# Loading the parameters of a state-space layer in whole tensors, with five neighbouring channels per partition

## The chip, the core and the metric

The kernel runs on one core of a Trainium2 chip. A core has five engines that work on their own instruction queues in order: PE (TensorE, matrix products into the PSUM memory), DVE (VectorE, elementwise work), ACT (ScalarE, functions by table, and copies), POOL (GpSimd) and SP (SyncE, which here only issues DMAs). ACT and POOL issue DMAs too. The transfers of all queues are carried out by the same 16 DMA engines. The metric is the device time of one launch in microseconds (us), less is better.

## The reference

Two branches read the same x (2048 positions, 640 channels, bfloat16). Branch a is an attention with 32 heads over 8 positions at distance 2. Branch b is a long convolution per channel, whose filter K comes from a state-space model with 192 complex states per channel. A gate mixes them.

```python
g = sigmoid((x * gate_w).sum(-1))
a = attention(x, wqkv, wo)                  # window 8, dilation 2, 32 heads
dt = exp(log_dt)[:, None]                   # 640 channels
logdA = dt * (A_re + 1j * A_im)             # 640 x 192
dB = dt * (B_re + 1j * B_im)
P = exp(logdA[:, :, None] * l)              # l = 0..2047
K = einsum("dn,dnl,dn->dl", C, P, dB).real
b = irfft(rfft(x, 4096) * rfft(K, 4096))[:2048] + x * Dskip
out = g * a + (1 - g) * b
```

The six parameter tensors (real and imaginary parts of A, B and C) are 640 x 192 in bfloat16, 245,760 bytes each.

## The kernel before

**Parameters.** A partition holds five of the 640 channels. Channel d = 80a + 16k + b (a below 8, k below 5, b below 16) lies in partition 16a + b, place k. So the five channels of a partition are 16 apart in memory, and a load of one place k moves 128 rows of 384 bytes (`load`, L294 to L297). There are thirty such loads, on SP, ACT and POOL. Those of place 0 of all six tensors come first. `lg10` (L298) is a 10 x 128 tile with log_dt and gate_w, which a small PE product (L321) turns into columns; ACT takes exp of the one half (`dtb`, L322) and copies the other (`gw_sb`, L324). On SP's queue the first of four DMA transposes of x (`xl`, L65) stands between the loads of cim and of aim. POOL issues five loads of the attention weights (`wl`, L66).

**The two parts.** `part` (L326) works out, for a block of places, what the filter needs: logarithm of the size, angle by arctangent, and the two exponents, and writes them as sums of bfloat16 pieces into `Sprm` in DRAM. Part one has place 0 alone (tiles of 128 x 192), part two the places 1 to 4 (128 x 768). Its steps are named after what they do: `weights` (products of C and B), `phase` (A_im times dt, then `wrap` into one turn), `ratio`, `squares`, `size`, `signs`, `angle`, and the splits `st`, `sx`, `sl`, `sp`, `sa`. A split step (`piece`, L347) rounds a tile to bfloat16 on ACT (L352), issues its write on SP (L354, L356) and takes the rest on DVE (L358). Part one runs at once. Of part two, seven steps are issued before the chunk loop (L821), and the others one per tick of it (`tick_hook`, L840). The arctangent and the logarithm of part two are held back (`kg.between`) until the exponentials of chunk 0 are done, because each function needs its own table on ACT.

**The chunks.** Ten chunks of 16 channels per group make the filter. `load_L` (L451) reads pieces from `Sprm` with eight DMAs per chunk. PE forms arguments (`ar`, L480), ACT takes sines (`trg`, L491) and exponentials (`exq`, L498), DVE multiplies them (L521 to L523), PE sums over states (`kps`, L532). Chunk 0 starts with exponentials and goes on with sines. The ticks of this loop interleave the projection of x (`proj`, products on L116, evictions to `prj` on L118, stores on L120), the gate, and the attention (`core`). The attention's buffers lie in memory that the parameters give back when part two is done (`c1.close()`, then `load_wo`).

**The rest.** The filter is expanded, both filter and x go through a Fourier transform in two stages (L633, L720), are multiplied, and come back in two more (L749, L763). `chan(c, q)` says which column of a group's 160 channels belongs to chunk c and slot q; the inverse stage takes twenty groups of four columns (L744 to L753) in the chunk order and `x0` puts them in place.

**Order.** The program's scheduler places independent instructions of one engine by its own estimate of when they can start; within an engine they then run in that fixed order. `after` (L418) adds an order between two instructions without a semaphore.

Of the kernel before, what the change touches and what calls it, by code (L numbers as in the profile page):

```python
# [220 lines left out]
NST = 192  # L221
# [4 lines left out]
CQ = 8  # L226
NCH = 80 // CQ
# [10 lines left out]

def chan(c, q):

    return 8 * c + q


def _arg_consts():
# [36 lines left out]
class SSMParams:  # L281
# [5 lines left out]
    def loads(self, ctx, tc, A_re, A_im, B_re, B_im, C_re, C_im, log_dt, gate_w, ident, gw_sb, pa, xl, wl):  # L287

        nc = tc.nc
        self.pin = pin = ctx.enter_context(tc.tile_pool(name="sp_in", bufs=1))  # L290
        self.t = t = {}
        src = dict(cre=C_re, bre=B_re, cim=C_im, bim=B_im, aim=A_im, are=A_re)

        def load(eng, nm, k0, nk):  # L294
            t[nm, k0] = pin.tile([128, nk, NST], BF16, name=f"{nm}{k0}")
            for k in range(k0, k0 + nk):
                eng.dma_start(t[nm, k0][:, k - k0], src[nm].rearrange("(a k b) n -> k a b n", k=5, b=16)[k])  # L297
        lg10 = pin.tile([10, 128], BF16, name="lg10")  # L298
        nc.sync.dma_start(lg10[0:5], log_dt.rearrange("(a k b) -> k a b", k=5, b=16))
        for nm in ("cre", "cim", "aim"):  # L300
            load(nc.sync, nm, 0, 1)
        for nm in ("bre", "bim", "are"):
            load(nc.scalar, nm, 0, 1)
        nc.sync.dma_start(lg10[5:10], gate_w.rearrange("(k p) -> k p", p=128))
        for nm in ("bre", "bim"):
            load(nc.scalar, nm, 1, 4)
        load(nc.sync, "cre", 1, 4)
        load(nc.sync, "cim", 1, 4)
        xl[0]()
        for w_ in wl:  # L310
            w_()
        load(nc.sync, "aim", 1, 4)
        load(nc.gpsimd, "are", 1, 4)
        for x_ in xl[1:]:
            x_()
        self.eps = pin.tile([128, 1], F32, name="eps")
        nc.vector.memset(self.eps[:], 1e-30)
        self.dtb = pin.tile([128, 5], BF16, name="dtb")
        self.dt2 = pin.tile([128, 5], F32, name="dt2")
        lt = pa.tile([128, 2, 512], F32, name="ar")  # L320
        nc.tensor.matmul(lt[:, 0, 0:10], lg10[:], ident[0:10, 0:10], start=True, stop=True)  # L321
        nc.scalar.activation(self.dtb[:], lt[:, 0, 0:5], ACT.Exp)  # L322
        nc.vector.tensor_tensor(self.dt2[:], self.dtb[:], self.dtb[:], ALU.mult)
        nc.scalar.activation(gw_sb[:], lt[:, 0, 5:10], ACT.Identity)  # L324

    def part(self, pool, tc, k0, nk, hold):  # L326

        nc = tc.nc
        SH = [128, nk, NST]
        cre, cim, bre, bim, are, aim = (self.t[n, k0][:] for n in ("cre", "cim", "bre", "bim", "are", "aim"))  # L330
# [5 lines left out]
        V, SCA = nc.vector, nc.scalar  # L336
# [5 lines left out]
        def wrap(dst, src, mul, tmp):  # L342
            V.tensor_scalar(tmp[:], src[:], float(mul / 65536.0), MAGIC, ALU.mult, ALU.add)
            V.tensor_scalar(tmp[:], tmp[:], MAGIC, 65536.0, ALU.subtract, ALU.mult)
            V.scalar_tensor_tensor(dst[:], src[:], float(mul), tmp[:], ALU.mult, ALU.subtract)

        def piece(cur, nxt, i):  # L347
            if pc1 is None:
# [13 lines left out]
            return [lambda i=i: piece(bufs[i], bufs[i + 1], i0 + i) for i in range(n)]  # L362
        TT = V.tensor_tensor
        def weights():
            TT(wr[:], cre, bre, ALU.mult)
            TT(t0[:], cim, bim, ALU.mult)
            TT(wi[:], cre, bim, ALU.mult)
            TT(t1[:], cim, bre, ALU.mult)
            TT(wr[:], wr[:], t0[:], ALU.subtract)
            SCA.activation(ax[:], wr[:], ACT.Abs)  # L370
            TT(wi[:], wi[:], t1[:], ALU.add)
            SCA.activation(ay[:], wi[:], ACT.Abs)

        def phase():
            TT(tau[:], aim, dtB, ALU.mult)
            wrap(tau, tau, U16, s0)

        def ratio():
            TT(t0[:], ax[:], ay[:], ALU.max)
            V.tensor_scalar(t0[:], t0[:], 1e-30, None, ALU.max)  # L380
            V.reciprocal(t0[:], t0[:])
            TT(t1[:], ax[:], ay[:], ALU.min)
            TT(t1[:], t1[:], t0[:], ALU.mult)
            hold(lambda: SCA.activation(at[:], t1[:], ACT.Arctan))
# [17 lines left out]
        def angle():  # L402
            q = float(np.pi / 4)
            S3 = V.scalar_tensor_tensor
            S3(t1[:], at[:], q, ax[:], ALU.subtract, ALU.mult)
            S3(t1[:], t1[:], q, wr[:], ALU.subtract, ALU.mult)
            S3(t1[:], t1[:], 2.0 * q, wi[:], ALU.add, ALU.mult)
            S3(at[:], t1[:], float(U16 / 124.0), tau[:], ALU.mult, ALU.add)
            wrap(at, at, 124.0, t1)
        st, sx, sa, sl, sp = split(tau, 0, 3), split(x1, 5, 3), split(xa, 3, 2), split(xl_, 10, 2), split(at, 8, 2)  # L410
        if nk > 1:
            return [weights, phase, squares, st[0], ratio, size, signs, st[1], st[2], lambda: wrap(x1, tau, 256.0, t0), sx[0], sx[1], sx[2],
                    sl[0], sl[1], angle, sp[0], sp[1], lambda: TT(xa[:], are, dtB, ALU.mult), sa[0], sa[1]]
        return [weights, phase, squares, st[0], ratio, size, signs, st[1], st[2], lambda: wrap(x1, tau, 256.0, t0), sl[0], sl[1], sx[0],
                sx[1], angle, sx[2], lambda: TT(xa[:], are, dtB, ALU.mult), sp[0], sp[1], sa[0], sa[1]]


def after(tc, later, earlier):  # L418
# [259 lines left out]
def fft_conv(ctx, tc, P, kx, gaS, out2d):  # L678
# [61 lines left out]
    with tc.tile_pool(name="ff_ps3", bufs=4, space=PSUM) as ps3, tc.tile_pool(name="ff_psr2", bufs=1, side="right") as psr2, \  # L740
# [44 lines left out]
def gated_mix_kernel(ctx, tc, A_x, A_wqkv, A_wo, B_A_re, B_A_im, B_B_re, B_B_im, B_C_re, B_C_im, B_log_dt, B_Dskip, gate_w, out):  # L785
# [37 lines left out]
    Dk = keep.tile([128, 160], BF16, name="Dk")  # L823
    nc.gpsimd.memset(Dk[:], 0.0)
    for g in range(4):
        nc.gpsimd.dma_start(Dk[32 * g:32 * g + 1], B_Dskip[160 * g:160 * g + 160].unsqueeze(0))
    Dk = Dk[:].rearrange("p (c x q) -> p c x q", c=2, q=CQ)
# [128 lines left out]
```

## Time and profile before

| what | value |
|---|---|
| time, three runs | 445.99, 449.24, 454.27 us; median 449.24 |
| the profiled execution | 449.92 us, span 448.1 us |
| busy PE, DVE, ACT, POOL (share of the span) | 336.5 (75%), 312.9 (70%), 324.8 (72%), 87.0 (19%) |
| weight loads of PE | 188.4 us (42%), beside the products |
| mean granted clock of PE | 0.926 of full speed |
| DMA moved | 58.80 MB, mean 131 GB/s |
| first product of the projection | 26.71 us |
| first exponential, first sine of chunk 0 | 52.05 us, 69.05 us |
| last Fourier products of chunk stage (L720) to the end | about 366 to 448 us |

The span runs from the first to the last instruction; the time has 1.8 us more around it. A row of a timeline gives start, length, engine, line, operation, tiles and count, and in brackets the idle time before it with what ended it. SPq, ACTq and POOL rows of the form DMA_DIRECT2D are issues, not the transfers: an issue can be long because its queue waits. A wait is put down to the release that came last.

### The profile page before, as it was taken

How to read it: one execution, taken by the hardware profiler on the slowest of the kernel's cores; microseconds unless marked ns; L12 is line 12 of the kernel's file. 1: busy time of each engine (PE TensorE's matmuls, PEld its weight loads, DVE VectorE, ACT ScalarE, POOL GpSimd, SP SyncE). 2: the span in 40 equal slices, each digit the busy share in tenths (PEclk: the TensorE clock that was granted, in tenths of full speed). 3: DMA queues.
4: the chain of work that ended last, by engine and by line, in shares of the span. 5: the costliest groups of instructions: out<-in, count | busy, mean ns of one | idle time of the engine just before them, and what ended most of it. 6: DMA issues, size and time to landing. Idle time of an engine off the chain costs nothing.

```text
span 448.1 us, 11301 instructions
## 1 busy us (share of the span) xinstructions
PE 336.5 (75%) x4806; PEld 188.4 (42%) x4806; DVE 312.9 (70%) x409; ACT 324.8 (72%) x485; POOL 87.0 (19%) x125
## 2 busy tenths in 40 slices
PE   0035867959988989799859998877867688995981
PEld 0012422424434435344325453534445565553871
DVE  0289937427998775767987759693545856999784
ACT  0258799847886788956838779968793649996784
POOL 8801211263130320231220210000000000000035
PEclk9995996988889999989998999989996979998897
DMA  7696443685455537182583641401207794213137
GB/s 238 138 178 169 147 130 121 178 246 160 115 146 134 135 85 180 58 228 68 186 233 103 187 144 25 115 11 16 77 1 220 264 177 86 82 37 119 71 67 170
DMA packets 66745, 58.80 MB, mean 131 GB/s; under 512 B 53303, under 2 KB 58599, under 8 KB 66439
## 3 DMA queue, kind: packets, MB, share of 16 engines
q1 hardware_dynamic: 56719, 29.26, 26.4%
q0 software_dynamic: 8176, 26.94, 21.0%
q10 hardware_dynamic: 1800, 1.88, 1.4%
q8 instruction: 37, 0.61, 0.6%
q14 instruction: 13, 0.11, 0.1%
HBM read 35.67 MB, written 19.77 MB: 124 GB/s over the span
## 4 chain that ended last, share of the span: by engine, by line
PE 36%; ACT 19%; DVE 13%; DMA 10%; issue 7%; POOL 1%; SPq 1%; ACTq 0%; POOLq 0%; DVEq 0%
PE tb L116 7%; PE tb L196 6%; PE fp L720 4%; PE tb L206 4%; PE ar L480 4%; DVE bufA L674 3%; DMA kc<-kS 3%; PE bp L633 3%; ACT exq L498 3%; ACT sp_u L723 2%; PE lg L163 2%; DVE prod L161 2%; ACT sp_k L723 2%; ACT prj L118 2%; ACT ga L207 2%
## 5 line engine op out<-in xcount | busy, mean ns | idle before, releaser
L491 ACT ACTIVATE trg<-ar 128x608 bf16<-128x608 int16 x120 | 76.9, 681 | 5.4 <-PE ar L480 4.8
L480 PE MATMUL ar<-Rarg,L 64*128 64x216 bf16 (+1 forms) x480 | 59.4, 285 | 16.3 <-ACT trg L491 9.8
L116 PE MATMUL tb<-bufA 128*128 128x512 bf16 x220 | 59.9, 403 | 2.3 <-ACT prj L118 1.4
L161 DVE TENSOR_TENSOR prod<-qc,kc 128x2048 bf16<-128x2048 bf16 x40 | 47.8, 1219 | 17.4 <-DMA L<-Sprm 7.9
L193 DVE TENSOR_TENSOR pv<-vc,asb 128x4096 bf16<-128x4096 bf16 (+1 forms) x24 | 45.7, 1928 | 19.7 <-DMA asb<-aS 17.2
L116 PEld LDWEIGHTS <-bufA 128*128 128x128 bf16 x300 | 33.4, 123 | 60.4 <-issue 40.8
L498 ACT ACTIVATE exq<-ar 128x864 bf16<-128x864 f32 x60 | 52.0, 904 | 0.5 <-PE ar L480 0.2
L196 PE MATMUL tb<-pv,ident 128*128 128x512 bf16 (+1 forms) x192 | 44.6, 372 | 3.6 <-DVE pv L193 1.8
L116 PE MATMUL lg<-bufA 128*128 128x512 bf16 x80 | 23.4, 429 | 26.7 <-DMA bufA<-in_A_x_dram 16.0
L532 PE MATMUL kps<-qq,pt 128*32 128x22 bf16 (+1 forms) x2560 | 37.5, 175 | 6.1 <-DVE E L884 2.3
L480 PEld LDWEIGHTS <-L 64*128 64x128 bf16 x480 | 22.1, 94 | 47.1 <-issue 42.4
L118 ACT ACTIVATE prj<-tb 128x512 bf16<-128x512 f32 x44 | 26.5, 601 | 21.0 <-PE tb L116 13.4
L532 PEld LDWEIGHTS <-pt 128*32 128x32 bf16 (+1 forms) x2560 | 25.2, 91 | 34.4 <-issue 26.2
L521 DVE TENSOR_TENSOR pt<-trg,exq 128x1024 bf16<-128x1024 bf16 x30 | 20.6, 686 | 20.2 <-ACT exq L498 10.4
L720 PEld LDWEIGHTS <-PHI 128*128 128x128 bf16 x256 | 24.8, 97 | 18.2 <-issue 8.1
L163 PE MATMUL lg<-prod,ind 128*32 128x512 bf16 x160 | 22.7, 417 | 11.5 <-DVE prod L161 8.0
L206 PE MATMUL tb<-wo_sb,oT 128*128 128x320 bf16 x160 | 26.9, 298 | 2.7 <-ACT ga L207 1.5
L196 PEld LDWEIGHTS <-ident 128*128 128x128 bf16 x192 | 18.7, 102 | 22.6 <-issue 11.2
L523 DVE TENSOR_TENSOR qq<-trg,exq 128x1408 bf16<-128x1408 bf16 x30 | 26.5, 884 | 0.0
L651 POOL DMA_DIRECT2D PHI<-c_phi x8 | 4.4, 548 | 112.6 <-PE fp L720 109.4
L197 ACT ACTIVATE oT<-tb 128x512 bf16<-128x512 f32 (+1 forms) x24 | 12.7, 529 | 18.0 <-PE tb L196 17.9
L207 ACT ACTIVATE ga<-tb,g_sb 128x320 bf16<-128x320 f32 x32 | 17.1, 534 | 9.1 <-PE tb L206 8.1
(182 smaller groups left out, 590.2 us busy)
## 6 DMA issues: line engine op xcount, KB each, us to landing
asb<-aS SPq DMA_DIRECT2D x8, 512.0 KB
PSI<-c_psi SPq DMA_DIRECT2D x8, 512.0 KB
PHI<-c_phi POOLq DMA_DIRECT2D x8, 384.0 KB, 3.6
L<-Sprm SPq DMA_DIRECT2D x80, 36.0 KB
kc<-kS POOLq DMA_DIRECT2D x8, 337.5 KB, 6.5
vc<-vS POOLq DMA_DIRECT2D x8, 337.5 KB, 5.8
qc<-qS POOLq DMA_DIRECT2D x8, 320.0 KB, 4.4
Usb<-in_A_x_dram POOLq DMA_DIRECT2D x4, 640.0 KB, 7.3
```

The lines of the kernel that those rows point to most:

```text
L116: nc.tensor.matmul(ppf, self.wq[:, kt, which * D + e:(which + 1) * D:5], self.xT[:, kt, c0:c0 + SC], start=(kt == 0), stop=(kt == NKT - 1))
L118: nc.scalar.activation(t[:, e % 2, :], ppf, ACT.Identity)
L161: nc.vector.tensor_tensor(prod[:], qc[:, e, :].unsqueeze(1).to_broadcast([128, W, C]), win(kc[:, e, :], 0, W, DIL, C), ALU.mult)
L163: nc.tensor.matmul(lg[32 * b:32 * b + 32], ind[:], prod[:, :, 64 * b:64 * b + 64], start=(e == 0), stop=(e == 4), skip_group_check=True, t ...
L193: nc.vector.tensor_tensor(pv[:, :, 0:n, :], for_e, asb[:].unsqueeze(2).to_broadcast([128, W, n, C]), ALU.mult)
L196: nc.tensor.matmul(op[:, 0:n, :], ident[:], pv[:, w, 0:n, :], start=(w == 0), stop=(w == W - 1))
L206: nc.tensor.matmul(apf[:, :320], oT[:, e, i * 128:(i + 1) * 128], wo_sb[:, e, hf * 320:(hf + 1) * 320], start=(e == 0), stop=(e == 4))
L480: nc.tensor.matmul(ar[:, g2, a0:a0 + ncol], L[rows, gp, sub, m0:m0 + 128], R[rows, c0:c0 + ncol], start=True, stop=True, tile_position=(64 ...
L491: ins = nc.scalar.activation(dst[:, 2 * gp:2 * gp + 2, sub, :], ar[:].bitcast(I16)[:, :, 0:2 * SW:2], ACT.Sin, scale=SCL)
L498: self.last = nc.scalar.activation(dst[:, 2 * gp:2 * gp + 2].rearrange("p g s n -> p g (s n)"), ar[:, :, 0:2 * EW], ACT.Exp)
L532: nc.tensor.matmul(kps[32 * g:32 * g + 32, c2, NM * ql:NM * ql + NM], pt[rows, 8 * g + ql, v, :], qq[rows, 8 * g + ql, v, :], start=(key n ...
L720: nc.tensor.matmul(fp[:, fl, 0:320].rearrange("p (c x) -> p c x", x=32), PHI[:, fl, kind, :], B[:, :, 2 * f1 + ri].rearrange("p c q g -> p ...
```

## The change

The channel order changes so that partition p holds the channels 5p to 5p + 4. A whole tensor then loads with one DMA of 128 rows of 1920 bytes. Six such loads stand on SP and ACT, three each; log_dt comes by a load of 128 rows of 10 bytes and needs no product; gate_w keeps the small product, and its load now follows the first transpose of x. The places 0 and 1 to 4 become slices of the loaded tiles. Those DVE instructions of part two that read inputs are ordered behind the last wrap of part one's `angle` (`behind`). The steps of part two come in another order, and two maxima in `ratio` become one instruction.

```diff
 def chan(c, q):
-    return 8 * c + q
+    return 40 * (c % 2) + 5 * q + c // 2
+
+def place(x):
+    return 8 * (2 * (x % 5) + x // 40) + x // 5 % 8
...
-        def load(eng, nm, k0, nk):
-            t[nm, k0] = pin.tile([128, nk, NST], BF16, name=f"{nm}{k0}")
-            for k in range(k0, k0 + nk):
-                eng.dma_start(t[nm, k0][:, k - k0], src[nm].rearrange("(a k b) n -> k a b n", k=5, b=16)[k])
...
+        def load(eng, nm, ap):
+            t[nm] = pin.tile([128, 5, NST], BF16, name=nm)
+            eng.dma_start(t[nm][:], ap.rearrange("(p k) n -> p k n", k=5))
+        ldt = pin.tile([128, 5], BF16, name="ldt")
+        lg5 = pin.tile([5, 128], BF16, name="lg5")
+        nc.sync.dma_start(ldt[:], log_dt.rearrange("(p k) -> p k", k=5))
+        load(nc.sync, "cre", C_re); load(nc.scalar, "bre", B_re)
+        load(nc.sync, "cim", C_im); load(nc.scalar, "bim", B_im)
+        load(nc.sync, "aim", A_im); load(nc.scalar, "are", A_re)
         for w_ in wl:
             w_()
-        load(nc.sync, "aim", 1, 4)
-        load(nc.gpsimd, "are", 1, 4)
+        xl[0]()
+        nc.sync.dma_start(lg5[:], gate_w.rearrange("(k p) -> k p", p=128))
         for x_ in xl[1:]:
             x_()
...
+        nc.scalar.activation(self.dtb[:], ldt[:], ACT.Exp)
+        nc.vector.tensor_tensor(self.dt2[:], self.dtb[:], self.dtb[:], ALU.mult)
         lt = pa.tile([128, 2, 512], F32, name="ar")
+        nc.tensor.matmul(lt[:, 0, 0:5], lg5[:], ident[0:5, 0:5], start=True, stop=True)
+        nc.scalar.activation(gw_sb[:], lt[:, 0, 0:5], ACT.Identity)
...
         def weights():
-            TT(wr[:], cre, bre, ALU.mult)
-            TT(t0[:], cim, bim, ALU.mult)
-            TT(wi[:], cre, bim, ALU.mult)
-            TT(t1[:], cim, bre, ALU.mult)
+            for dst, p, q in ((wr, cre, bre), (t0, cim, bim), (wi, cre, bim), (t1, cim, bre)):
+                after(tc, TT(dst[:], p, q, ALU.mult), behind)
...
         def ratio():
-            TT(t0[:], ax[:], ay[:], ALU.max)
-            V.tensor_scalar(t0[:], t0[:], 1e-30, None, ALU.max)
+            V.scalar_tensor_tensor(t0[:], ax[:], 1e-30, ay[:], ALU.max, ALU.max)
...
         if nk > 1:
-            return [weights, phase, squares, st[0], ratio, size, signs, st[1], ...]
+            return [weights, ratio, squares, size, phase, st[0], signs, st[1], ...]
...
-    psteps = prm.part(pB, tc, 1, 4, kg.between.append)
+    psteps = prm.part(pB, tc, 1, 4, kg.between.append, prm.last)
...
-                        nc.tensor.matmul(cp[:, c2, l, :], Y[64 * c2:64 * c2 + 64, ro, 4 * cb + l, :],
+                        nc.tensor.matmul(cp[:, c2, l, :], Y[64 * c2:64 * c2 + 64, ro, place(4 * cb + l), :],
...
-            x0 = chan(cb // 2, 4 * (cb % 2))
-            dst = C.rearrange("p x (c q) -> p x c q", c=2)[:, :, :, x0:x0 + 4]
+            dst = C.rearrange("p x (c q) -> p x c q", c=2)[:, :, :, 4 * cb:4 * cb + 4]
...
+    for c2_ in range(2):
+        nc.gpsimd.tensor_copy(Dk[:, c2_].rearrange("p (j s) q -> p j s q", s=2), Dn[:, 80 * c2_:80 * c2_ + 80].rearrange("p (s q j) -> p j s q", s=2, j=5))
```

`Dn` takes the place of `Dk` as the target of the Dskip loads, and the two POOL copies bring it into the new channel order. `self.last` is the last instruction of part one's `angle`; phase and the A_re product of part two are put behind it in the same way.

More of the change, by code (lines that the diff above doesn't have):

```diff
@@ L291, in loads @@
         self.t = t = {}
-        src = dict(cre=C_re, bre=B_re, cim=C_im, bim=B_im, aim=A_im, are=A_re)
-        def load(eng, nm, k0, nk):
-            t[nm, k0] = pin.tile([128, nk, NST], BF16, name=f"{nm}{k0}")
-            for k in range(k0, k0 + nk):
[L297 to L309, printed above, removed]
+        def load(eng, nm, ap):
[7 more added lines that the diff above has]
+        load(nc.sync, "aim", A_im); load(nc.scalar, "are", A_re)
         for w_ in wl:
             w_()
-        load(nc.sync, "aim", 1, 4)
-        load(nc.gpsimd, "are", 1, 4)
+        xl[0]()
+        nc.sync.dma_start(lg5[:], gate_w.rearrange("(k p) -> k p", p=128))
         for x_ in xl[1:]:
@@ L319, in loads, with part @@
         self.dt2 = pin.tile([128, 5], F32, name="dt2")
+        nc.scalar.activation(self.dtb[:], ldt[:], ACT.Exp)
+        nc.vector.tensor_tensor(self.dt2[:], self.dtb[:], self.dtb[:], ALU.mult)
         lt = pa.tile([128, 2, 512], F32, name="ar")
[L321 to L326, printed above, removed]
+        nc.tensor.matmul(lt[:, 0, 0:5], lg5[:], ident[0:5, 0:5], start=True, stop=True)
+        nc.scalar.activation(gw_sb[:], lt[:, 0, 0:5], ACT.Identity)
+    def part(self, pool, tc, k0, nk, hold, behind=None):
         nc = tc.nc
         SH = [128, nk, NST]
-        cre, cim, bre, bim, are, aim = (self.t[n, k0][:] for n in ("cre", "cim", "bre", "bim", "are", "aim"))
+        cre, cim, bre, bim, are, aim = (self.t[n][:, k0:k0 + nk] for n in ("cre", "cim", "bre", "bim", "are", "aim"))
         f = lambda nm: pool.tile(SH, F32, name=f"{nm}_{k0}")
@@ L344, in wrap @@
             V.tensor_scalar(tmp[:], tmp[:], MAGIC, 65536.0, ALU.subtract, ALU.mult)
-            V.scalar_tensor_tensor(dst[:], src[:], float(mul), tmp[:], ALU.mult, ALU.subtract)
+            return V.scalar_tensor_tensor(dst[:], src[:], float(mul), tmp[:], ALU.mult, ALU.subtract)
         def piece(cur, nxt, i):
@@ L374, in phase @@
         def phase():
-            TT(tau[:], aim, dtB, ALU.mult)
+            after(tc, TT(tau[:], aim, dtB, ALU.mult), behind)
             wrap(tau, tau, U16, s0)
         def ratio():
-            TT(t0[:], ax[:], ay[:], ALU.max)
-            V.tensor_scalar(t0[:], t0[:], 1e-30, None, ALU.max)
+            V.scalar_tensor_tensor(t0[:], ax[:], 1e-30, ay[:], ALU.max, ALU.max)
             V.reciprocal(t0[:], t0[:])
@@ L408, in angle @@
             S3(at[:], t1[:], float(U16 / 124.0), tau[:], ALU.mult, ALU.add)
-            wrap(at, at, 124.0, t1)
+            self.last = wrap(at, at, 124.0, t1)
         st, sx, sa, sl, sp = split(tau, 0, 3), split(x1, 5, 3), split(xa, 3, 2), split(xl_, 10, 2), split(at, 8, 2)
         if nk > 1:
-            return [weights, phase, squares, st[0], ratio, size, signs, st[1], st[2], lambda: wrap(x1, tau, 256.0, t0), sx[0], sx[1], sx[2],
-                    sl[0], sl[1], angle, sp[0], sp[1], lambda: TT(xa[:], are, dtB, ALU.mult), sa[0], sa[1]]
+            return [weights, ratio, squares, size, phase, st[0], signs, st[1], st[2], lambda: wrap(x1, tau, 256.0, t0), sx[0], sx[1], sx[2],
+                    sl[0], sl[1], angle, sp[0], sp[1], lambda: after(tc, TT(xa[:], are, dtB, ALU.mult), behind), sa[0], sa[1]]
         return [weights, phase, squares, st[0], ratio, size, signs, st[1], st[2], lambda: wrap(x1, tau, 256.0, t0), sl[0], sl[1], sx[0],
-                sx[1], angle, sx[2], lambda: TT(xa[:], are, dtB, ALU.mult), sp[0], sp[1], sa[0], sa[1]]
+                sx[1], angle, sx[2], lambda: after(tc, TT(xa[:], are, dtB, ALU.mult), behind), sp[0], sp[1], sa[0], sa[1]]
 def after(tc, later, earlier):
@@ L822, in gated_mix_kernel @@
         psteps.pop(0)()
-    Dk = keep.tile([128, 160], BF16, name="Dk")
-    nc.gpsimd.memset(Dk[:], 0.0)
+    Dk = keep.tile([128, 2, NCH, CQ], BF16, name="Dk")
+    Dn = keep.tile([128, 160], BF16, name="Dn")
+    nc.gpsimd.memset(Dn[:], 0.0)
     for g in range(4):
-        nc.gpsimd.dma_start(Dk[32 * g:32 * g + 1], B_Dskip[160 * g:160 * g + 160].unsqueeze(0))
-    Dk = Dk[:].rearrange("p (c x q) -> p c x q", c=2, q=CQ)
+        nc.gpsimd.dma_start(Dn[32 * g:32 * g + 1], B_Dskip[160 * g:160 * g + 160].unsqueeze(0))
+    for c2_ in range(2):
+        nc.gpsimd.tensor_copy(Dk[:, c2_].rearrange("p (j s) q -> p j s q", s=2), Dn[:, 80 * c2_:80 * c2_ + 80].rearrange("p (s q j) -> p j s q", s=2, j=5))
     kx = KExpand(ctx, tc, Dk)
```

## The prediction

> **What bounds the kernel now.** I read the slices first, then the chain of waits, then the timelines of the opening. The slices:
>
> ```profile
> PE   0035867959988989799859998877867688995981
> DVE  0289937427998775767987759693545856999784
> ACT  0258799847886788956838779968793649996784
> ```
>
> One slice is 11.2 us. From the third on, three engines share the load and none is full; in the first two PE does nothing and ACT almost nothing. Each engine works in its written order, so a later stage starts when the earlier one lets it. The change touches the opening, so its worth is read there. The chain of waits, followed back, ends in it:
>
> ```profile
> 54.16 0.78 ACT exq L498
> 63.45 1.28 ACT L384
> 67.76 1.28 ACT L491
> 82.31 6.83 DMA Sprm<-pc
> 91.57 5.87 DMA kc<-kS
> ```
>
> Columns are start, length, what. The first piece is an exponential of chunk 0. From there to the attention's first loads at 91.57 the chain runs over the parameters: their table loads (L384, L491), the write of the last piece, and loads into the memory that they free. So what comes before 54 us is waited for. The timelines of the opening (start, length, engine, line, tile) show how it is made:
>
> ```profile
> 3.80 7.27 SPq L297 DMA_DIRECT2D cre<-in_B_C_re_dram  x4
> 18.88 4.59 SPq L65 DMA_TRANSPOSE bufA<-in_A_x_dram  x1
> ...
> 43.80 7.57 SPq L458 DMA_DIRECT2D L<-Sprm  x16
> ```
> ```profile
> 18.44 1.28 ACT L322 ACT_TABLE_LOAD   x1 [18.44 <-DMA bim<-in_B_B_im_dram]
> ...
> 27.50 0.36 ACT L352 ACTIVATE pc<-s 128x192 bf16<-128x192 f32 x1 [1.11 <-DVE s L358]
> ...
> 52.05 0.89 ACT L498 ACTIVATE exq<-ar 128x864 bf16<-128x864 f32 x1
> ```
> ```profile
> 12.17 0.36 DVE L366 TENSOR_TENSOR t<-cim,bim 128x192 f32<-128x192 bf16 x1 [7.81 <-DMA bim<-in_B_B_im_dram]
> 23.99 0.96 DVE L367 TENSOR_TENSOR wi<-cre,bim 128x768 f32<-128x768 bf16 x1 [3.61 <-DMA bim<-in_B_B_im_dram]
> ```
>
> ACT and SP spend the opening issuing thirty small parameter loads: SP needs 7.27 us for four, and ACT gets to its first table load at 18.44. DVE then reaches a product of the second part (four channels) at 20.4 and stands 3.61 us for bim, with the first part's wrap behind it. The milestones that I carry are: ACT's second rounding of the first part (27.50), the end of that part (the last split at 41.1), the L loads (43.80), the first exponential (52.05), and, from the same view of ACT, the first sine at 69.05.
>
> ```profile
> 27.50:41.10 13.60, 5.09 (x14) 1.87 (x13) 13.60 (x34) 12.81 (x25) 0.31 (x1) 0.71 0.87 181
> 52.05:69.05 17.00, 10.05 (x55) 4.52 (x54) 8.11 (x10) 16.92 (x22) 1.99 (x3) 0.95 0.33 99
> ```
>
> Busy time in two stretches (PE, weight loads, DVE, ACT, POOL, clock, DMA share, GB/s): the first is bound by DVE, the second by ACT.
>
> **The loads.** Thirty loads of 128 x 384 bytes become six of 128 x 1920; the bytes stay 1.47 MB. The issues cost about 0.6 us each, so ACT has three instead of eleven and is free near 4 us instead of 18.4, SP near 3.3. Against that, the first part used 0.29 MB and now needs whole tensors, which arrive under the attention weights (2.46 MB, issued by POOL from 2.48 us). In the trace a packet of 384 bytes takes 22 ns, one of 1920 bytes (another load's) 89 ns and the weights' packets of 7680 bytes 313 ns. 768 x 89 and 320 x 313 over 16 DMA engines are 4.3 + 6.3 = 10.6 us, so all has landed at 13.1 if it starts at 2.5. The other bound is the rate of 4 to 12 us, 302 to 329 GB/s: 3.93 MB less 0.29 moved by 4 us, at 315, ends at 15.6. I take 14. For aim, last in its queue, I assume no place better than the end.
>
> How queues share the engines decides between the ends. The row is the first bim block: issued at 2.80, waited for until 12.17, though it is 128 packets, 0.2 us of sixteen engines. The Trainium skill (DMA: Bandwidth & Descriptors, Queues, rings and completion order) says that each DMA engine takes turns between queues a packet at a time, a packet being some 9 to 17 descriptors. By that a tensor's eight descriptors per engine would pass in one turn, and the third tensor of a queue would come three of the weights' long turns later: it speaks against the change, at the late end or beyond. No row here shows a turn's length.
>
> **x and the gate.** The first transpose of x now stands behind aim on SP's queue, and the gate weights (lg5) behind that transpose. The changed order shows more: PE's small product for the gate stands behind the first projection matmul, and its eviction gw_sb stands on ACT ahead of the first part's second rounding. So everything behind it on ACT (both table loads, all later splits) waits for x. That is a new wait. The transpose's packets took 4.8 us beside other loads and 2.9 to 3.6 alone; I take 3.2 after 14, then 1.5 us to the first matmul (packets ended at 25.2, PE began at 26.71) and 0.8 for two products and the eviction: gw_sb at 19.5, bounds 17.5 and 21.5. Before, ACT did that second rounding at 27.50. Meanwhile weights, phase and the wrap of the first part hide under the loads; with that cover gone they would cost some 3 us.
>
> **First part.** In the 13.60 us stretch DVE did 7.9 us of the second part (eight products or sums at 0.87 and two at 0.47, spaced). The new order puts all of these behind the first part, so 5.7 us of its own remain as the lower bound. But five projection evictions now stand between its splits on ACT, with PE groups of 1.24 to 2.3 us behind them, so the old 13.6 is the upper one. I take the middle, 9.6: end at 29.1. SP has issued the three other transposes by then (3.2 us each from 17.2 is 26.8). The writes and their landing cost 2.7 as before (41.1 to 43.80): L loads at 31.8.
>
> **First exponential.** Before it came 8.25 us after the L loads began, with PE ready after 6.5 (49.98 plus a product of 0.36) and an eviction and a table load in between that can now go earlier. I take 7.0: 38.8.
>
> **Exponential to first sine.** ACT is full there, 17 us, and now has more in it: nine projection evictions instead of six (0.49 each) and six roundings plus one sign instead of four plus one (0.8 each), 3.1 us; with PE's pace for groups in a row up to 5. I take 3.5: first sine at 59.3 instead of 69.05. The second part's own chain on DVE lies beside this: by its rows some 19 us of passes with the 4.86 us reciprocal, 5 for the next wrap and splits, 3 of waits for ACT's roundings, 27 in all; from 27 it is at its arctangent at 54.
>
> **Edits at nothing.** The fused maximum saves a pass (0.47) on an engine with slack there. The two Dk copies (80 columns each) sit on POOL between projection stores that wait for ACT anyway; their loads go out with those stores, with 5.6 us to land, ahead of the k stores, and exposed would cost up to 5 us of POOL. chan and place alter addresses only: same shapes, same strides, same counts. From the arctangent on, the order on every engine is the same in both kernels, table loads included (24), so I carry the gain to the end.
>
> **Sum.** 69.05 - 59.3 = 9.75 us. The profiled execution took 449.92 (span 448.1), 0.7 over the median 449.24: 440.2 against it; I say 440.0. The own range from gw_sb (2 each way), first part (up to 3.9) and exponential stretch (1.5), not all at one end, is 436 to 444.5.
>
> **Rivals.** (1) The parameters hardly wait for the weights: larger packets take more of every turn, aim is there at 11, gw_sb at 17, the splits run near their 5.7 plus two table loads of 1.28. Then the sine comes at 55 to 56, and the time is 435 to 437. For it: from 5 to 12 us the trace has 394 parameter packets of 384 bytes beside about 270 of the weights, so what a turn carries decides. Against: DMA was 98% busy from 8 to 12, so bytes must come from the weights, which the first projection needs. (2) The gain is absorbed: the attention's loads at 91.57 wait for the last write and wo, and the long middle is shared by three engines; 446 to 450. Against: identical orders. (3) Slower: the weights hold the whole tensors back, and with them x, the gate and all of ACT's queue, while "behind" forbids DVE to fill the gap with second-part work. Each us by which gw_sb comes after 19.5 takes one from the gain: nothing is won at 29.3, and over 2% (9 us) lost past 38. Three tensors follow each other on a queue; if each takes bim's 9.4 us, aim is there at 31 and gw_sb at 36.5, and with the slower ends of the later steps the time is 459 to 462. For it: that bim row. Against: the weights' last packet starts at 12.7 in this trace, and all bytes fit before 15.6. That the change does nothing is excluded, since thirty issues go.
>
> **How the numbers follow.** A measurement here can tell about 2% from no change (three runs spread from 445.99 to 454.27); faster means under 440.3. Forecast 0.60, just over half of it beyond the bound (0.34 faster, 0.26 same). Rival 1: 0.24, faster. Rival 2: 0.05, same. Rival 3: 0.11, slower. So 0.58, 0.31, 0.11. The range 434 to 449 takes in forecast and rival 1 with their bounds and part of rival 2, and leaves out some 0.15.
>
> **What would show it.** ACT's first table load near 4 us; the first wrap at 14 to 16; gw_sb directly after the first projection matmul, at 17.5 to 21.5; L loads at 30 to 34; first sine at 57 to 62. From there each milestone should keep its distance to the end: the last Fourier stages, 364 to 411 before, move by the same amount. I am wrong if aim lands after 18, if DVE rather than ACT is late at the second arctangent, or if the distance from sine to end changes by over 3 us.

## The result and the profile after

The changed kernel took 447.08 us (median of 20 runs, 440.33 to 454.24), the kernel before 450.79 (20 runs, 445.99 to 454.65). The ratio is 0.9897, its 95% interval 0.9854 to 0.994. So it is 3.7 us faster, less than 2% and less than half of the 9.75 us that were forecast. Three more series of both, made later (after5, after6 and after7), gave 5.2, 4.5 and 5.0 us between the medians, about half of the forecast. The profiled execution took 447.28 us, span 445.5.

A ratio here is of the faster runs of each kernel alone; where a single early run of the kernel before (442.25 and 441.07 us in two series) makes it leave out most of its others, medians of all runs are compared.

The slices of the profile after, 11.1 us each, granted clock of PE below:

```profile
PE   0458749788889897998659998797768589995980
DVE  4399673279998848679668759664557557998882
ACT  2478999649977989668329689788775468995882
PEclk9997959969999999899859999979996889998896
```

The first two slices are fuller now: DVE is busy for 0.4 of the first one, where it had nothing to do before, and PE starts in the second slice and not in the third. The chain of waits (start, length, what) begins with the transposes of x and still runs over the parameters to the attention's first loads; its last line here lies far behind the opening:

```profile
2.67 11.17 SPq L65
13.89 3.61 DMA lg<-in_gate_w_dram
...
58.74 1.28 ACT L485
...
73.88 5.47 DMA Sprm<-pc
...
82.08 6.42 DMA kc<-kS
...
212.80 11.60 DMA kc<-kS
```

The attention's loads come at 82.08 in place of 91.57, 9.5 us earlier. Before, the line that answers to the last one was this, in the same view:

```profile
223.12 7.71 DMA kc<-kS
```

There the load was 10.3 us later, but it took 3.9 us less. The opening in the timelines of SP, ACT and DVE (start, length, engine, line, tile; idle time in brackets):

```profile
2.67 11.17 SPq L65 DMA_TRANSPOSE bufA<-in_A_x_dram  x1
...
24.23 4.29 SPq L353 DMA_DIRECT2D Sprm<-pc  x5
30.80 7.49 SPq L452 DMA_DIRECT2D L<-Sprm  x16
```
```profile
2.64 1.28 ACT L317 ACT_TABLE_LOAD   x1 [2.64 <-issue]
...
17.77 0.18 ACT L321 ACTIVATE gw_sb<-ar 128x5 bf16<-128x5 f32 x1 [6.15 <-PE ar L320]
...
37.30 0.89 ACT L492 ACTIVATE exq<-ar 128x864 bf16<-128x864 f32 x1
...
60.04 0.68 ACT L485 ACTIVATE trg<-ar 128x608 bf16<-128x608 int16 x1
```
```profile
6.43 0.36 DVE L363 TENSOR_TENSOR t<-cim,bim 128x192 f32<-128x192 bf16 x1 [1.14 <-DMA bim<-in_B_B_im_dram]
...
8.08 0.36 DVE L370 TENSOR_TENSOR tau<-aim,dtb 128x192 f32<-128x192 bf16 x1
```

ACT's first table load is at 2.64 in place of 18.44, and DVE uses aim, the last tensor, at 8.08. The second row of ACT shows the new wait: it is for PE, whose first product waits for x. The first sine comes at 60.04 in place of 69.05.

To see where these 9 us went, I set the two traces against each other, instruction by instruction on DVE and ACT. The lead is 9 us at the first sine, 9.1 to 11.3 from 120 to 225 us of the time before, and 6.5 at 231. From there it goes on falling, to 4.1 at 340 us, and the closing of the kernel takes 1.4 more (below), so that the spans differ by 2.6. Two rows of DVE mark the large step, at 231. Before:

```profile
231.02 1.22 DVE L161 TENSOR_TENSOR prod<-qc,kc 128x2048 bf16<-128x2048 bf16 x1 [1.16 <-DMA kc<-kS]
```

After:

```profile
224.52 1.22 DVE L161 TENSOR_TENSOR prod<-qc,kc 128x2048 bf16<-128x2048 bf16 x1 [5.34 <-DMA kc<-kS]
```

The same product waits 5.34 us for its load in place of 1.16. Windows around it, the middle one from some 2 us behind the first of the filter's loads, show what it draws with it (us, then busy time of PE, weight loads, DVE, ACT and POOL, granted clock, DMA share, GB/s), after:

```profile
169.60:214.50 44.90, 39.38 (x603) 18.71 (x601) 34.79 (x51) 33.33 (x53) 10.75 (x14) 0.96 0.46 138
214.50:234.50 20.00, 11.47 (x206) 5.21 (x206) 12.11 (x15) 7.03 (x11) 2.58 (x3) 0.66 0.58 170
234.50:295.00 60.50, 53.43 (x917) 26.88 (x915) 47.24 (x51) 49.69 (x78) 5.42 (x8) 0.94 0.32 93
```

and before:

```profile
180.00:225.00 45.00, 39.47 (x620) 18.81 (x618) 35.42 (x52) 33.67 (x53) 10.76 (x14) 0.96 0.45 136
225.00:240.00 15.00, 9.66 (x206) 4.97 (x206) 11.34 (x14) 6.91 (x11) 2.58 (x3) 0.89 0.78 226
240.00:300.00 60.00, 52.84 (x921) 27.16 (x920) 47.33 (x52) 49.85 (x78) 5.42 (x8) 0.97 0.33 95
```

The same 206 products of PE take 20 us in place of 15, the stretches around them are alike, and PE was granted 0.66 of its clock there in place of 0.89. PE's busy time grew by only 1.8 us, so most of the 5 us is waiting.

What meets there: at the end of chunk 4 the expanded filter is read back with four loads kc<-Kx of 327 KB (two on ACT, two on SP, packets of 10,240 bytes), and the attention reads its next keys with kc<-kS on POOL (packets of 4,320 bytes). All are issued within 1.4 us. In the kernel before, kc<-kS is issued 0.42 us after the first kc<-Kx and ahead of SP's first one (0.56); in the changed kernel at 0.77, behind it. Its first packet then moves at 3.87 us in place of 2.45, and that of SP's first one at 3.51 in place of 3.99. The opposite order of two issues is 0.35 us of difference at POOL and 4 us at DVE in these two executions.

### The profile page after: what moved, and what is told of

It is laid out like the page before. It is cut to its first block, busy times and chain, and to the rows that moved or that the text cites. A ratio compares the mean times of both kernels' runs of the same rounds, so it can differ in the third digit from the quotient of the medians.

```text
span 445.5 us, 11261 instructions
## 1 busy us (share of the span) xinstructions
PE 338.7 (76%) x4806; PEld 188.3 (42%) x4806; DVE 314.8 (71%) x407; ACT 324.6 (73%) x485; POOL 87.8 (20%) x123
## 4 chain that ended last, share of the span: by engine, by line
PE 39%; ACT 21%; DVE 16%; DMA 13%; issue 5%; SPq 4%; POOL 1%; ACTq 0%; DVEq 0%; POOLq 0%
PE tb L116 8%; PE tb L196 6%; PE fp L714 4%; PE tb L206 4%; PE ar L474 4%; DMA kc<-kS 4%; DVE bufA L668 3%; PE bp L627 3%; SPq L65 3%; ACT sp_u L717 2%; PE lg L116 2%; PE lg L163 2%; DVE prod L161 2%; ACT sp_k L717 2%; ACT prj L118 2%
## 5 line engine op out<-in xcount | busy, mean ns | idle before, releaser
L474 PE MATMUL ar<-Rarg,L 64*128 64x216 bf16 (+1 forms) x480 | 60.9, 289 | 24.2 <-ACT trg L485 11.4
L116 PE MATMUL tb<-bufA 128*128 128x512 bf16 x220 | 61.5, 409 | 2.2 <-ACT prj L118 1.2
L193 DVE TENSOR_TENSOR pv<-vc,asb 128x4096 bf16<-128x4096 bf16 (+1 forms) x24 | 45.7, 1927 | 21.5 <-DMA asb<-aS 17.6
L196 PE MATMUL tb<-pv,ident 128*128 128x512 bf16 (+1 forms) x192 | 43.5, 365 | 3.8 <-DVE pv L193 2.0
L515 DVE TENSOR_TENSOR pt<-trg,exq 128x1024 bf16<-128x1024 bf16 x30 | 20.5, 685 | 18.5 <-ACT exq L492 10.4
L196 PEld LDWEIGHTS <-ident 128*128 128x128 bf16 x192 | 18.5, 101 | 22.5 <-issue 10.1
L197 ACT ACTIVATE oT<-tb 128x512 bf16<-128x512 f32 (+1 forms) x24 | 12.7, 529 | 20.6 <-PE tb L196 20.5
```

Source lines behind the costliest of these rows:

```text
L116: nc.tensor.matmul(ppf, self.wq[:, kt, which * D + e:(which + 1) * D:5], self.xT[:, kt, c0:c0 + SC], start=(kt == 0), stop=(kt == NKT - 1))
L193: nc.vector.tensor_tensor(pv[:, :, 0:n, :], for_e, asb[:].unsqueeze(2).to_broadcast([128, W, n, C]), ALU.mult)
L196: nc.tensor.matmul(op[:, 0:n, :], ident[:], pv[:, w, 0:n, :], start=(w == 0), stop=(w == W - 1))
L474: nc.tensor.matmul(ar[:, g2, a0:a0 + ncol], L[rows, gp, sub, m0:m0 + 128], R[rows, c0:c0 + ncol], start=True, stop=True, tile_position=(64 ...
```

## The experiments

**Chance or not.** First both kernels again, unchanged.

> The changed kernel once more, as it is, for a second profile. In its first profile the first sine of chunk 0 came 9.0 us earlier than before, the lead was 10.7 us at 225 us of the old time, and 4.2 of it went between 225 and 240: there one attention load (kc from kS, 12.80 to 24.52 after 200) took 11.6 us instead of 7.7 beside four filter loads (kc from Kx), and PE ran 13.7 us at half clock behind it. Theory 1 (the loss is a fixed consequence of the new timing): the same load takes 11 to 12 us again and the stretch from the seventh k store's load to the next attention score is as long as in the first profile, 20 us. Rival (the loss is a matter of chance per execution): the load takes 7 to 9 us in this profile, the lead after it is 9 to 10.5 us, and what is lost lies elsewhere or nowhere. First sine in both: 59.5 to 60.5 us.

> The kernel of before once more, for a second profile. Theory 1: the load of kc from kS at 223 us takes 7.5 to 8 us again, and stages keep the lengths of the first profile within 0.5 us. Rival (chance): this load varies here too, by 2 us or more, or half-clock stretches of PE lie elsewhere and move a stage by 2 us or more. First sine at 68.5 to 69.5 in both.

443.33 and 450.9 us. I take as measure the stretch from the 26th to the 31st of DVE's products `prod`: 22.7 us in the first execution of the changed kernel and 22.0 here, 18.6 in both of the kernel before. So the lengthening is no chance of one execution. The first sine of the kernel before came at 66.90 this time; the 69.05 on which the forecast stands was a late one.

**The gate.** Is `gw_sb` what the opening waits for, as the prediction has it?

```diff
+        nc.sync.dma_start(lg5[:], gate_w.rearrange("(k p) -> k p", p=128))
         load(nc.sync, "cre", C_re); load(nc.scalar, "bre", B_re)
...
-        nc.sync.dma_start(lg5[:], gate_w.rearrange("(k p) -> k p", p=128))
```

> One change to the changed kernel: the load of gate_w goes out on SP right behind log_dt, ahead of the parameters and x, so that the gate's product and the eviction gw_sb no longer wait for the first transpose of x (ACT stood 6.15 us for it). Opening: gw_sb before 11 us, the first part's end 5 to 6 us earlier than 28 us unless the three later transposes on SP hold its writes (they end at 24.1), then only about 3 us earlier: L loads at 26 to 28 instead of 30.8, first sine at 55 to 58 instead of 60.0. End: theory A (a lead of the opening is carried to the end, minus chance) gives a time 2 to 4 us below the changed kernel, 443 to 445; theory B (the middle takes a lead back, whatever its size) gives the changed kernel's time within 1 us.

`gw_sb` was written at 4.04 in place of 17.77, and little came of it: the first part's last rounding came 0.8 us earlier (27.05), the first sine 0.7 (59.39), the L loads later (31.17, not 30.80). The time was 447.62 us, ratio 0.9895 (0.9826 to 0.9964). ACT's timeline shows why:

```profile
4.04 0.16 ACT L321 ACTIVATE gw_sb<-ar 128x5 bf16<-128x5 f32 x1
...
14.16 0.36 ACT L349 ACTIVATE pc<-s 128x192 bf16<-128x192 f32 x1 [1.11 <-DVE s L355]
...
21.67 0.60 ACT L118 ACTIVATE prj<-lg 128x512 bf16<-128x512 f32 x1 [2.79 <-PE lg L116]
```

The second rounding is early now, but the first eviction of the projection stands on ACT ahead of the rest of the splits, and that waits for x as before. PE's first product came 1.6 us later here (18.32, not 16.73), so the two kernels differ in x too.

**The order of the two loads.** A semaphore is a counter by which one instruction waits for another. Each DMA of POOL signals its end on one of eight, taken in turn. The kernel before has four more DMAs on POOL (are) than the changed one, so all later ones have other semaphores. The load kc<-kS waits for five of them, one after the other, and where the last one to come (that of POOL's last store of keys) stands in that row decides when the load is issued. In the kernel before it stands last, and the load goes out 0.28 us after the store has landed (223.12 and 222.84); in the changed kernel it stands first, and the load goes out 0.63 us after (212.80 and 212.17). Four tiny loads shift the turn by four, with the same order of everything else on every engine:

```diff
+        scr = pin.tile([4, 16], BF16, name="scr")
+        for k in range(4):
+            nc.gpsimd.dma_start(scr[k:k + 1], gate_w[0:16].unsqueeze(0))
```

> The changed kernel with four tiny loads more on POOL's queue (16 elements of gate_w each, into a tile nobody reads), right behind the loads of wl. Nothing is left out of the computation, and the order of the rest on every engine is as in the changed kernel. What moves is which of its rotating completion semaphores each later DMA of POOL signals; with four more they fall as in the kernel before. Theory A (the lead is lost because the load kc<-kS of the attention comes behind the filter's loads kc<-Kx, and this comes from the order in which POOL's wait on four semaphores is worked off): kc<-kS is issued at +0.4 to +0.5 us after the first kc<-Kx (changed kernel +0.77), before SP's first kc<-Kx at +0.56; VectorE's waiting product starts at +8 to +9 (changed +11.7 to +12.5); the stretch from the 26th to the 31st product takes 18.4 to 19.2 us (changed 22.0 to 22.8, before 18.6); the time falls by 3 to 4 us to 443 to 444.5. Theory B (the lead is lost whatever the order, because the loads are bound by what they carry and the filter's start sets the end): issue or not, the stretch stays at 22 to 23 us and the time at 447 +- 1. Theory C (the order flips back, the stretch is short, but the gain is given back in the next 100 us since three engines share the middle): stretch 18.4 to 19.2, time 446 to 447.5.

> The kernel before with the same four tiny loads on POOL's queue at the same place, and nothing else; orders as before. Theory A: the semaphores now fall as in the changed kernel, so kc<-kS is issued at about +0.77 us, behind SP's first kc<-Kx, the stretch from the 26th to the 31st product grows from 18.6 to 22 to 23 us, and the time by 3 to 4 us to 454 to 455. Theory B (the flip belongs to the rest of the change, not to the semaphores): issue at +0.4 to +0.5, stretch 18.6, time 451 +- 1. Theory C: stretch 22 to 23, time 451 to 452.

The changed kernel with them: 443.84 us (12 runs); the kernel before with them: 452.74 (6 runs); the kernel before beside both: 450.51. So the kernel before lost 2.2 us between the medians, where theory A had 3 to 4; the changed kernel as it is was not run beside them. In the trace of b_sw4 the issue moved from 0.42 to 0.77 and the stretch from 18.6 to 21.6, as theory A has it, though only the semaphores moved with the four tiny loads:

```profile
230.54 1.23 DVE L161 TENSOR_TENSOR prod<-qc,kc 128x2048 bf16<-128x2048 bf16 x1 [4.25 <-DMA kc<-kS]
```

In a_sw4 the stretch was 17.3, shorter than expected, since in this execution the filter's loads came late of themselves (3.5 us after POOL's last store of keys, not 1.9). All profiled executions with the loads in this place, measured from that store:

| executions | kc<-kS issued | first kc<-Kx issued | 26th to 31st product | 26th product to 17th `pv` |
|---|---|---|---|---|
| before, b_again, b_cp2 | 2.31 to 2.37 | 1.89 | 18.5 to 18.6 | 49.0 |
| b_sw4 | 2.67 | 1.89 | 21.6 | 52.9 |
| after, a_again, after5, after7, a_gate, a_nobehind | 2.66 to 2.70 | 1.89 | 22.0 to 22.9 | 52.6 to 54.1 |
| a_nb_sw4, a_rows4 | 2.31 | 1.89 | 18.6 to 18.7 | 49.0 to 50.6 |
| a_sw4, a_best, after6 | 2.31 to 2.67 | 3.36 to 3.52 | 17.3 | 50.6 to 51.7 |

So the semaphores set when kc<-kS goes out, and where the filter's loads come at 1.89 that sets the stretch, in both kernels and both ways. The last row shows another case: when the filter's loads come 1.5 us later, kc<-kS is free of them, but the attention's stores and loads behind it are caught. DVE in after6, the changed kernel:

```profile
231.35 0.69 DVE L178 TENSOR_TENSOR at<-lgs,rs 128x512 bf16<-128x512 f32 x1 [2.58 <-DMA aS<-at]
235.21 4.49 DVE L193 TENSOR_TENSOR pv<-vc,asb 128x4096 bf16<-128x4096 bf16 x2 [3.16 <-DMA asb<-aS]
```

These two waits, 5.7 us, stand in place of the 5.34 for kc<-kS.

**The ordering of the second part.**

```diff
-    psteps = prm.part(pB, tc, 1, 4, kg.between.append, prm.last)
+    psteps = prm.part(pB, tc, 1, 4, kg.between.append)
```

> The changed kernel without the ordering of the second part's first reads behind the first part's last rounding (the argument behind is left out), so the scheduler may put products of the second part into the first part's waits on VectorE. Theory A says this ordering is no part of the loss at the load kc<-kS: that stretch stays at 22 to 23 us, and only the opening may move: with the first part ending at 27.8 +- 2 and the first sine at 60 +- 2, time 446 to 449. Rival (the ordering costs VectorE the first part's idle time, which the second part could have used): first sine at 56 to 58, time 443 to 445. Third way (without it the second part's work comes ahead of the first part's, and the first part ends later): first part's end at 30 to 34, first exponential later than 38.5, time 449 to 453.

444.73 us (10 runs), first sine at 58.7, first exponential at 42.2, the stretch at 22.3. The last is as theory A says. For the opening it looked like the rival, 1.4 us earlier than the changed kernel; but in a_nb_sw4, which has the same opening and four tiny loads, the sine came at 60.7. What `behind` is worth stays open within some 2 us.

**Both, and the end of the kernel.** In the changed kernel the last store's packet moves 17 us after the first product of the last stage, as in the kernel before, but the end comes 3.4 us after that packet in place of 1.9. In the trace it is POOL's closing drain that ends late: 5.78 us long in place of 3.55. I suspected the copies of Dk on POOL (a_nb_sw4 joins the four tiny loads with the second part set free; a_best is a_nb_sw4 with the copies on DVE; b_cp2 adds the copies on POOL to the kernel before).

```diff
-        nc.gpsimd.tensor_copy(Dk[:, c2_].rearrange(...), Dn[...])
+        nc.vector.tensor_copy(Dk[:, c2_].rearrange(...), Dn[...])
```

> The changed kernel as it is, beside the next three on one chip. Stretch from the 26th to the 31st product 22 to 23 us, POOL's closing drain 5.5 to 6 us long (before 3.6 to 3.9), time 446 to 448, before 450 to 452.

> The changed kernel with both edits: the four tiny loads on POOL's queue, and the second part without its ordering behind the first. Nothing is left out. If the two gains are apart (theory A: one is a race of loads at chunk 4, the other VectorE's and ScalarE's idle time in the opening), the first sine is at 58.5 to 59.5, the stretch from the 26th to the 31st product at 17.4 to 19, and the time 2 to 3 us below the kernel with the four loads alone (443.84): 440.5 to 442.5. Rival (they overlap: what the opening gives is lost by the filter's start, whose wait is the same in both): 443 to 445.

> The last kernel with the two copies of Dk on VectorE in place of POOL. Nothing is left out. Theory P (a copy anywhere on POOL lengthens POOL's closing drain, which ends the kernel 1.4 us later after the last store than in the kernel before): drain 3.5 to 4 us long, the end 1.2 to 1.6 us nearer to the last store's packet, time 1 to 1.5 us below the last kernel. Rival (the drain's length follows from where POOL's last stores are issued, or from anything else in the change): drain 5.5 to 6 us, time the same as the last kernel's or 0.3 us above, the copies' time on VectorE.

> The kernel before with the two copies of Dk on POOL, into a tile nobody reads, at the place that they have in the changed kernel. Theory P: POOL's closing drain ends about 2.5 us after the last store's packet in place of 1.1, and is 5.5 to 6 us long in place of 3.55, time 1.4 us above before. Rival: drain as in the kernel before (ends at 1.1 us), time the same.

445.07, 444.47 and 444.37 us (12 runs each), and 450.53 for b_cp2 (one run); the kernel before had 450.22. Two expectations fell. The drain was 5.66 without copies on POOL (a_best) and 3.64 with them (b_cp2): the copies don't make it. And a_nb_sw4 has the short stretch (18.7) but is 0.6 us below the changed kernel beside it, with a spread of 7 us in each: the 4 us of the stretch are not seen in the time. It lost 3.01 us to asb<-aS further on.

**Rows on POOL's queue.** The four loads again, now with 128 rows of 384 bytes each, as those of are had.

```diff
+        scr = pin.tile([128, 4, NST], BF16, name="scr")
+        for k in range(4):
+            nc.gpsimd.dma_start(scr[:, k], A_re.rearrange("(a k b) n -> k a b n", k=5, b=16)[k + 1])
```

> The changed kernel with four loads more on POOL's queue, now of the size that the four left-out loads of are had (128 rows of 384 B each, from A_re, into a tile nobody reads). Nothing is left out. The lanes fall as in the kernel before, and so does the number of descriptors that POOL has written by the end. Theory R (POOL's closing drain depends on how many rows its queue has carried): POOL's wait between its 11th and 12th store is back (issue at 12.3 us behind the first product of the last stage in place of 11.5), the drain is 3.5 to 4 us long in place of 5.7 to 5.9, the end 1.7 to 1.9 us behind the last packet in place of 3.3; the stretch from the 26th to the 31st product 17.4 to 19; time 443 +- 1. Rival (the drain belongs to another part of the change, the rows of the channels or the smaller code): drain 5.7 us, end 3.3 us behind the last packet, time 444.5 +- 1.

The drain is 3.68 and the end 2.0 us after the last packet: theory R. POOL's stores in the last stage, the changed kernel and then a_rows4:

```profile
434.47 1.16 POOL L770 DMA_DIRECT2D out_dram<-ot  x2 [0.37 <-DVE ot L767]
436.00 3.46 POOL L770 DMA_DIRECT2D out_dram<-ot  x6 [0.38 <-DVE ot L767]
```
```profile
431.81 0.58 POOL L773 DMA_DIRECT2D out_dram<-ot  x1 [0.38 <-DVE ot L770]
433.23 1.16 POOL L773 DMA_DIRECT2D out_dram<-ot  x2 [0.84 <-issue]
434.58 1.73 POOL L773 DMA_DIRECT2D out_dram<-ot  x3 [0.19 <-issue]
```

With the rows the last six stores are issued in three groups with gaps, without them at a stretch; the later issue goes with the earlier end. Four loads of one row (a_sw4) leave the drain at 5.76, so it is the rows or their bytes, not the number of loads. Why, no run shows. In the time, 444.53 against 448.25, the 1.4 us can't be told from the scatter.

**The meeting taken away.** If the loads that meet are the loss, both kernels with the filter's loads one chunk later must keep the opening's lead.

```diff
+                if c == HC:
+                    half["kc"] = kx.load(0, kk)
                 if cl == HC - 1:
                     kx.expand(hf, E, kk, pk, kg.S12)
-                    if hf == 0:
-                        half["kc"] = kx.load(0, kk)
```

> The changed kernel with the filter's first four loads kc<-Kx issued one chunk later, at the end of chunk 5, so that they do not meet the attention's load kc<-kS. Nothing is left out; the order of the middle is another one than in the changed kernel (and the same other one as in the next run). Theory A' (the lead of 9 us at the 26th product is lost to the meeting of the loads and its followers): against the next run the lead is kept: 7 to 8 us less than it at the end. Theory C (the middle gives back any lead whatever meets there; what is kept is 4 to 5.5 us): 4 to 5.5 us less than it.

> The kernel before with the same move of the filter's first loads. It is the measure for the run ahead of it; by itself: 450 +- 4.

> The changed kernel with both: the filter's first loads one chunk later, and the four loads of rows more on POOL's queue. Nothing is left out. If the two losses are apart (the meeting of the loads 3 to 4 us, the closing drain 1.4 us), this is 4.5 to 5.5 us below the next run, and 0.5 to 2 us below the run with the filter's loads alone (440.87): 439 to 440.5 where before is 448 to 450. Rival (they overlap, or the order of the middle was luck): 441 to 443.5. POOL's closing drain 3.5 to 4 us.

> The changed kernel as it is, as the measure beside the run ahead of it: 443.5 to 447, and 4 us below before.

440.87 us (6 runs) against 449.10 (12 runs): 8.2 apart, or 7.8 with a 95% interval of 5.9 to 9.7 from the means. The changed kernel beside a_final, which has the rows on POOL too, took 444.78, a_final 441.31; its ratio to the kernel before is 0.9781 (0.9729 to 0.9832). The rows added nothing that the time shows. The two profiled executions of the pair were only 4.5 us apart, so the pair was run again with the changed kernel beside it.

> The changed kernel with the filter's first four loads one chunk later, again, now beside the changed kernel itself and the other half of the pair. The timed runs said 8.2 us between the pair, the two profiled executions 4.5. Theory A' (the lead of the opening is kept when the loads do not meet): 7 us or more below the next run, 3 to 4.5 us below the run after it. Theory C (the middle gives any lead back, and the first pair's 8.2 was scatter): 4 to 5.5 us below the next run, 0 to 2 below the one after it.

> The kernel before with the same move, again: within 1 us of the kernel before by theory A' and by theory C, since there the loads met in the harmless order.

> The changed kernel as it is, beside the pair: 4 to 5 us below before.

443.01, 450.54 and 446.99 us, the kernel before 452.02. The pair is 7.5 apart (from the means 7.6, interval 4.7 to 10.5), the moved loads are worth 4.0 to the changed kernel (3.9 for the first a_kclate against after6, which ran in another series) and 1.5 or -0.9 to the kernel before. The profiled executions were 11.7 apart this time. That agrees with theory A': the opening's lead is kept when the loads don't meet; the 4 to 5.5 us of theory C lie outside the first interval, though not outside the second. The order of the middle differs from the changed kernel's in a_kclate, but it is the same in the pair. So the pair shows that the lead can be kept; that the other order of the middle has no part in it was not tried. These versions are the fastest of all: a_kclate and a_kclate2 have 0.9863 (0.982 to 0.9907) and 0.9835 (0.9778 to 0.9892) of the kernel before.

## Why the prediction was wrong

**The step that failed** is the last: "From the arctangent on, the order on every engine is the same in both kernels, table loads included (24), so I carry the gain to the end." The order on every engine is the same, but the order between engines is not. Three queues issue within 1 us at chunk 4, and which comes first is decided by semaphore turns that the four left-out loads of POOL had moved. A list of each engine's instructions can't show that. Moving the filter's loads away puts the price of the meeting at 3.9 and 4.0 us in the changed kernel; less what the same move does to the kernel before, that is 2.5 to 4.8.

The traces show the loss at that place in other executions too. Against the mean of before, b_again and b_cp2, five executions of the changed kernel lead by 8.6 us at the 26th product and by 4.3 at the 17th `pv`. The four with four loads more on POOL (a_sw4, a_nb_sw4, a_best, a_rows4) still lead there by 6.3 to 8.3. In the time this can't be told from the scatter: these four were 6.7, 5.8, 5.9 and 3.7 us faster than the kernel before beside them, the changed kernel 3.7 to 5.2. So how much of the price is the order alone, and how much the waits that follow further on, stays open. One of the prediction's own signs of being wrong came true as well: from the first sine to the end it took 385.5 us in place of 379.1, where 3 us of change were allowed. Over five and three executions the means are 383.6 and 380.8.

**The loads.** Assumed at 14 (13.1 to 15.6), with aim last. DVE used bim at 6.43 and aim at 8.08, the wrap began at 8.47 where I looked for 14 to 16. The DMA engines were 99% busy up to 27 us. But the parameters' 768 packets started between 2.26 and 8.09, and the weights' 320 between 6.55 and 13.07, where before these began at 3.83: the parameters hardly waited for the weights, as rival (1) had it. Why the weights began later, no run shows. My reading of the rule of the Trainium skill that I weighed (DMA: Bandwidth & Descriptors, Queues, rings and completion order) put the third tensor of each queue late; here it was not, but with no packet of the weights before 6.55 the loads hardly put the rule to the test.

**x and the gate.** `gw_sb` at 17.77 was inside 17.5 to 21.5 by luck, since two errors met: aim was there at 8 and not at 14, but the first transpose, on SP from 2.67, was through only at 13.84. Its packets met the weights': from 7 to 13 us 362 of its packets of 256 bytes started, beside 307 of the weights' 7680 bytes. And that each us of `gw_sb` is one of gain is wrong, at least for an earlier one, by a_gate; what binds is the first eviction of the projection, which hangs on the same x.

**First part, L loads, first exponential.** 27.82 for the last rounding, 30.80 and 37.30, where I had 29.1, 31.8 and 38.8. The middle values were right within 1.5 us.

**Exponential to first sine.** 22.74 us in place of 20.5; the evictions of the projection come with waits for PE between the exponentials, 0.7 beyond the slower of the two bounds (17 and 5). So the first sine at 60.04 (59.3).

**The starting point.** Over five executions of the kernel before with its opening unaltered the first sine came at 66.9 to 69.05, mean 67.9, and over seven of the changed kernel's at 59.7 to 61.4, mean 60.5: 7.4 us, where one execution of each says 9.0. Up to the 26th product these twelve have 8.5 us between them. Less 4.0 for the meeting of the loads that is 4.5, and the medians show 3.7 to 5.2. The drain's 1.4 would make it 3.1; the sums close within some 2 us, not better. So 2.3 of the 9.75 us were missing at the first sine already: 1.1 because the sine at 69.05 was a late one, 1.2 because the changed kernel's came later than 59.3.

**Edits at nothing.** The Dk copies were off the path (POOL at 29.30, 3.55 us) and are not what lengthens the drain. That fewer rows on POOL's queue could lengthen it I did not see.

**The rivals.** (2), the gain absorbed, had the right time, 446 to 450, and 0.05. The place it named was wrong: at the attention's first loads (82.08) the lead was still 9.5. Against it I had put "identical orders", which is the failed step again. (1) was right that the loads are early, though no run shows its reason, and wrong on the time, since the splits wait for x anyway. (3) did not come.

## What to carry to other kernels

A gain at the front can be lost where something behind it depends on how queues stand to one another; ahead of carrying it, look in the trace for places where several queues issue bulk loads within a microsecond, and for who waits on the small one among them. Leaving out DMAs moves the semaphores of all later ones on that queue, so timing at such places can change although every engine's order is the same. Take a first milestone from several executions before a forecast is made from it: one execution of this kernel was 1.1 us off its mean there.

## What was not expected of the hardware

- Two issues in the opposite order, 0.35 us apart in time, went with a stretch with the waiting product that is 3.0 to 4.4 us longer; SP's two loads with 10,240-byte packets then start ahead of the small one (3.51 and 3.87 us in place of 3.99 and 2.45).
- A wait for five semaphores is worked off one after the other. With the store landing 2.03 and 2.04 us after its issue, POOL issued the next load 2.66 us or 2.31 us after it, by the order alone.
- POOL's closing drain took 3.36 to 3.88 us in the kernels whose POOL queue had carried 512 rows more, and 5.46 to 6.03 in the others, with the later stores issued sooner in the latter.
- PE's granted clock falls to half for stretches of 3.4 to 13.7 us. In one execution of the changed kernel these add up to 75.3 us, in another to 61.7; its runs' times go with the granted clock in the first series (correlation -0.83 over 20 runs, about 3.4 us per 0.01), less so in the later ones (-0.49, 0.11 and -0.64 over 12, 6 and 10 runs). The changed kernel was granted 0.917 to 0.921 on average in its series, the kernel before 0.920 to 0.926. Whether that takes part of the gain wasn't tried.
